# A fused window attention and maxout FFN: the hand-listed order of all steps is replaced by another one

## Chip, cores and metric

The kernel runs on one NeuronCore of a Trainium2 chip. The metric is the device time of one execution in microseconds; of several executions the median is taken. Engines are called PE (TensorE), DVE (VectorE), ACT (ScalarE), POOL (GpSimd) and SP (SyncE, which only issues transfers here).

## The reference

```python
def _attn_ref(q, k, v):                  # 8 batches, 8 heads, 576 positions, 64 wide
    ...
    scores = scale * np.matmul(q, k.transpose(0, 1, 3, 2))
    rel = pos[:, None] - pos[None, :]
    mask_plain = (rel >= 0) & (rel < window)                                  # heads 0 to 3, window 32
    mask_dil = (rel >= 0) & (rel < window * dilation) & (rel % dilation == 0) # heads 4 to 7, dilation 4
    ...
    scores = scores - np.max(scores, axis=-1, keepdims=True)
    attn = np.exp(scores)
    attn = attn / (np.sum(attn, axis=-1, keepdims=True) + 1e-09)
    return np.matmul(attn, v).astype(np.float32)

def _moe_ref(x, w1, w2, w3, w_out):      # x: 4608 tokens x 512; w: 512 x 768; w_out: 768 x 512
    h = np.maximum(np.maximum(x @ w1, x @ w2), x @ w3)
    return (h @ w_out).astype(np.float32)
```

The attention's output, with the heads side by side, is the x of the FFN.

## The kernel before

Attention works on units of one batch and two heads (32 units). The first eight (`early`, from line 601) use blocks of 32 rows, the other 24 (`attention` and `behind`, from line 888) blocks of 64. A unit goes: loads, scores on PE (L649 or L922), maximum and mask on DVE (L677, L960), exponential on ACT (L692, L972), sums, reciprocal, normalization (a two-operand product W times sm on POOL or DVE, L488), 32x32 transposes on DVE (L741, L1026), values on PE (L760, L1082), and copies of the result out of PSUM.

The FFN takes 4608 tokens in six tiles (`TILES`: 512, 512, 768, 768, 1024, 1024). Every fp32 operand is split into a high part in fp32r, copied by ACT or POOL (L456, L458), and a low part, subtracted by DVE or POOL (L488); a product is then three matmuls. The two first tiles (`plain`, L1551 and L1490) use the weights as they come; the four later ones (`fast`, L1793, and `turned_down`, L1357) use a scheme of seven products of half matrices instead of eight, whose operands are sums and differences of blocks (`changed`, L488 again) and whose weight sums are made once (`sums_of`, `down_sums`), stored to HBM (`kept_up`, `kept_d`) and loaded again as they are used (L1753, tile `wup_a<-kept_up`). Weights arrive as 512 KB loads (`st<-in_w_up_dram`, step `weight`), and each is taken apart by POOL or DVE (L554), ACT (L549), DVE (L560), a copy and a subtraction. Lines that are helpers are `copy` (L456 ACT, L458 POOL, L460 DVE) and `tt` (L488), which makes all two-operand work on DVE and POOL.

All this is put down as 3121 steps (`Plan.add`), each with the engines that may do it, its dependences and its buffers. Their order is not worked out by the kernel: `Plan.order` reads it from the string `SEQUENCE` (line 60), one number for each step, the step's place in the order of `add`. A letter behind a number (a, d, p) is the engine ACT, DVE or POOL where it isn't the step's first choice; an `f` is a filler, one bf16 matmul on a block of zeros (L2016) that only keeps PE busy. Steps are issued in that order, so the order on every engine, and on SP's queue of transfers, is the order of the string. An engine does its steps in that order and no other. `SLOTS` fixes which buffer each step uses. `Plan.issue` also makes each of the first 36 loads wait until no more than 2 MB of loads before it are under way.

Steps that the text speaks of by number:

- 163, 181: values of the first two units on PE; 209: a score block; 234: the first FFN matmul
- 60: load of weight tile 10, taken apart by 62, 63; 48, 54, 72, 42: loads of tiles 8, 9, 12, 7; 576: load of q and k for the score block 578
- 401, 403, 405: parts of a weight sum on DVE; 119: low part of a down weight on DVE; 140: first part of a weight; 311: the maximum that frees a PSUM bank in the first tile
- 1106, 1113: low parts of the third tile's inputs on DVE; 1107, 1114: differences of its blocks on POOL; 531, 535: low parts of weight sums on POOL
- 1168: load of a weight sum in the third tile; 2106: load of q and k of a later unit, 592 KB
- 2136: the short normalization of a unit (64x192) on POOL; 1350, 1352: copies of the high parts that the P7 products of the third tile take; 1355: a low part for them; 1611, 1614, 2289: differences of 768 or 1024 columns for the next tile; 1612, 2293, 2297: copies of its inputs

Of the kernel before, what the change touches and what calls it, by code (L numbers as in the profile page):

```python
# [60 lines left out]
    "152 f 170 f 189 f 188 f f 150 f f f f 0 154 f 207 155 172 156 f f 6 173 f f f f 174 f f 2 1 153 f f 157 191 3 "  # L61
    "175 158 f 176 f 159 18 f f 12 f 160 192 177 f f 161 f 7 f 178 138 193 f f 8 162 171 194 209 179 9 195 10 163 24 "
    "180 f 11 14 f 190 f f 210 208 f 13 196 f 4p 144 f 164 211 f 168 5 166 165 212 169 167 151 181 19 197 213 20 36 "
    "214d 215 f 15 216 f 66 186 f 21 182 f f f 538 187 f 22 26 f 234 217 184 235 198 16 236 23 237 25 239 185 17 218 "
    "183 30 27 199 28p 225 243 223 78 245 367 219 247 224 221 227 238 220 248 244 366d 200 557 368d 222 370 228 246 "
    "203 205d 226 29 201 229 48 206 31 230 371d 251 249 202 32 540 204 42 369 33 233 376p 34 250 242 240 38 35 232 54 "
    "241 231 541 372p 378 252 253 254 373 256 257 255 258 260 37 261 259 262 264 72 39 44 374 263 377 265 43 40 45 60 "
    "559 49 41 50d 46 51 90 266 56 542 55 268 52p 267 57 126 543 382 269 375 47 58 544 270 61 62 272 383 108 271 63 "
    "273 576 53 59 274 560 67 68 276 561 73 84 64 277 275 80 379 69 545 278 74 70 546 75 280 96 65 562 539 547d 79 "
    "281 384 279 102 282 563 76p 81 386 578 71 86 284 85 387d 385 564d 283 77 285 388 87 82 390 286 91 92 114 83 88 "  # L70
    "597 288 98 97 287 132 389 93 289 565 579 94 290 104 392 391 99 292 393 580 100 291 293 548 103 399 395 294 95 "
    "581 120 394 105 89 109 296 396 295 106 598 297 582 110 747 412 107 298 398 577 116d 115 380 599 583d 381 299 566 "
    "584 111 300 600 122 301 117 101 585d 302 400 304 303 401d 121 305 118 128 123 127 306 601 402 124 308 129 125 "
    "307 130 309 403d 133 131 119d 310 139 408 312 134 410 140d 460 313 311 146 409 141 314 135 145 112 316 324 113d "
    "317 404 315 406 405d 318 602 749 147 414 411 320 567 148 142 407 136 603 549 325 319 321 586 558 415 322 137d "
    "149 328 550 143 552 329 551 554 553 556 417 330 323 604 555 587 336 416d 418d 326 419 331 594d 596 588 327p 332 "
    "420 595 591d 424 751 589 422 421 592 593 426 337 425 423 333 827 801 787 764 338 756 334 797 768 431 752 339 757 "
    "762 335 766 590 754 763 760 340 427 770 346 758 795 605 341 799 606 803 761 805 793 568 755 791 347d 753 432 829 "
    "789 342 607 748 430 571 569 343 771 570 759 348 572 776 356 344d 434 349 769 435d 575 608 804 433d 573d 767 440p "
    "777 765 574 350 609 617d 773 615d 796 357 351 436 612d 616 352 794 438 774 437d 800 353 442 775d 441 439 831 354 "  # L80
    "806 772 443 611 792 429 802 447 355 358 790 842 846 788 345 838 359 613 847 428 848 798 834 360 750 832 844 446d "
# [2019 lines left out]
```

## Time and profile before

| | us |
|---|---|
| median of 3 runs | 635.98 (634.64 to 637.69) |
| the profiled execution | 637.17 |
| its span, first to last instruction | 635.4 |
| PE, DVE, ACT, POOL busy | 621.5, 507.8, 312.8, 227.1 |
| mean granted clock of PE | 0.997 |

A wait of PE shows in two ways: as idle time with the name of what ended it, and inside the busy time, since the ends of matmuls are modelled; the distance between the starts of matmuls shows both. A wait of DVE or POOL that begins when the instruction has been started is part of that instruction's duration.

### The profile page before, as it was taken

The page shows a single profiled execution, that of the slowest core. Times are in us where ns is not written, and L with a number is a line of the kernel's source. Part 1 is how long each engine was busy: PE and PEld are TensorE (multiplying, and loading weights), DVE is VectorE, ACT ScalarE, POOL GpSimd, SP SyncE. Part 2 cuts the span into 40 slices and gives each one's busy share as a digit, 9 for nine tenths or more (in the row PEclk, how much of TensorE's full clock was granted, in tenths as well). Part 3 has the DMA queues.
Part 4 walks back from the last instruction along what each step waited for, and adds up shares of the span by engine and source line. Part 5 has one row for each costly group of instructions (what it writes and reads, how often), then busy time and mean ns, then how long its engine had stood idle before and what let it go on. Part 6 is the DMA issues. An engine that isn't in the chain of part 4 may idle for free.

```text
span 635.4 us, 16084 instructions
## 1 busy us (share of the span) xinstructions
PE 621.5 (98%) x6025; PEld 530.1 (83%) x6025; DVE 507.8 (80%) x1368; ACT 312.8 (49%) x935; POOL 227.1 (36%) x266
## 2 busy tenths in 40 slices
PE   9898999999999999999999999999999999999997
PEld 4576868888888999898999999788888888888886
DVE  7868999999899998799889899987668854327575
ACT  3445547575766573665337457543135632212153
POOL 3779978989777411254102012520000000000000
PEclk9899999999999999999999999999999999999999
DMA  8999956996598998957979894565746366765533
GB/s 298 304 303 297 361 185 240 320 348 213 189 330 260 318 337 276 327 174 237 312 235 303 274 324 162 166 215 163 241 152 197 117 210 200 273 189 166 172 128 133
DMA packets 79710, 153.24 MB, mean 241 GB/s; under 512 B 7952, under 2 KB 26384, under 8 KB 79632
## 3 DMA queue, kind: packets, MB, share of 16 engines
q1 hardware_dynamic: 79488, 151.94, 72.1%
q8 instruction: 48, 0.79, 0.5%
q14 instruction: 30, 0.25, 0.1%
q10 hardware_dynamic: 144, 0.26, 0.1%
HBM read 123.08 MB, written 29.10 MB: 240 GB/s over the span
## 4 chain that ended last, share of the span: by engine, by line
PE 80%; DVE 8%; DMA 8%; issue 2%; POOL 1%; ACT 1%; SPq 0%; DVEq 0%; POOLq 0%; ACTq 0%
PE ffn L1793 46%; PE ffn L1357 12%; PE ffn L1551 10%; PE ffn L1490 4%; DMA st<-in_w_up_dram 4%; PE pair L922 3%; PE pair L1082 3%; DVE hs_all L488 2%; DVE wup_a L488 2%; DMA kept_up<-wup_a 1%; PE ffn L2016 1%; DMA wup_a<-kept_up 1%; DMA fk<-in_qk_p_dram 1%; DMA fk<-in_qk_d_dram 1%; DVE PT L1026 1%
## 5 line engine op out<-in xcount | busy, mean ns | idle before, releaser
L1793 PE MATMUL ffn<-wup_a 128*128 128x384 f32 (+1 forms) x1188 | 236.2, 356 | 1.9 <-DMA wup_a<-kept_up 1.1
L1793 PEld LDWEIGHTS ffn<-wup_a 128*128 128x128 f32 x1188 | 211.4, 188 | 21.5 <-DVE wup_a L488 2.4
L1551 PE MATMUL ffn<-xs,wup_a 128*128 128x512 f32 x408 | 97.5, 395 | 2.6 <-DVE hf L488 2.5
L1551 PEld LDWEIGHTS ffn<-xs,wup_a 128*128 128x128 f32 x408 | 75.7, 188 | 20.3 <-DVE hf L488 3.8
L488 DVE TENSOR_TENSOR hf<-ffn,hf 128x512 f32<-128x512 f32 (+1 forms) x96 | 60.0, 632 | 25.3 <-PE ffn L1793 22.3
L1026 DVE STREAM_TRANSPOSE PT<-W 32x256 f32<-32x256 f32 (+2 forms) x192 | 77.1, 401 | 3.3 <-POOL W L488 0.2
L972 ACT ACTIVATE W<-W,mx 128x96 f32<-128x96 f32 (+2 forms) x180 | 65.7, 367 | 10.3 <-DVE mx L960 9.8
L996 POOL TENSOR_SCALAR sm<-sm 128x8 f32<-128x8 f32 (+2 forms) x48 | 12.4, 257 | 118.8 <-ACT W L972 72.8
L456 ACT COPY ffn<-ffn 128x384 f32<-128x384 f32 (+1 forms) x32 | 16.6, 520 | 68.3 <-PE ffn L1793 52.7
L1357 PE MATMUL ffn<-hs_all,wdn 128*128 128x512 f32 (+1 forms) x228 | 49.5, 365 | 0.8 <-DVE hs_all L488 0.7
L456 ACT CAST hs_all<-hf 128x384 fp32r<-128x384 f32 (+4 forms) x55 | 32.2, 589 | 33.3 <-PE ffn L1357 17.1
L1357 PEld LDWEIGHTS ffn<-hs_all,wdn 128*128 128x128 f32 x228 | 41.2, 188 | 6.4 <-DVE hs_all L488 1.3
L1793 PE MATMUL ffn<-wup_a,wdn 128*128 128x512 f32 x192 | 46.1, 391 | 0.0
L488 DVE TENSOR_TENSOR hs_all<-hf,hs_all 128x384 fp32r<-128x384 f32 (+3 forms) x55 | 39.0, 721 | 7.9 <-ACT hs_all L456 6.8
L488 POOL TENSOR_TENSOR W<-W,sm 128x768 f32<-128x768 f32 (+2 forms) x33 | 38.5, 1173 | 15.1 <-DVE sm L1001 14.5
L488 POOL TENSOR_TENSOR hf<-hf 128x256 f32<-128x256 f32 (+1 forms) x41 | 41.6, 1020 | 5.6 <-DVE hf L488 2.2
L1793 PEld LDWEIGHTS ffn<-wup_a,wdn 128*128 128x128 f32 x192 | 35.8, 188 | 7.6 <-DVE wup_a L488 0.2
L1357 PE MATMUL ffn<-hs_all,wup_a 128*128 128x384 f32 (+1 forms) x198 | 39.2, 352 | 0.8 <-DVE hs_all L488 0.8
L456 ACT COPY u<-ffn 128x384 f32<-128x384 f32 (+1 forms) x35 | 18.5, 530 | 42.9 <-PE ffn L1793 42.1
L458 POOL TENSOR_SCALAR hs_all<-PT 128x512 fp32r<-128x512 f32 x1 | 0.6, 621 | 106.8 <-PE ffn L1357 106.8
L1357 PEld LDWEIGHTS ffn<-hs_all,wup_a 128*128 128x128 f32 x198 | 35.0, 188 | 3.8 <-DVE hs_all L488 1.6
L1490 PE MATMUL ffn<-wdn,hs_all 128*128 128x512 f32 x144 | 34.9, 395 | 0.2 <-DVE hf L488 0.2
(207 smaller groups left out, 1051.8 us busy)
## 6 DMA issues: line engine op xcount, KB each, us to landing
wup_a<-kept_up SPq DMA_DIRECT2D x198, 256.0 KB, 4.4
st<-in_w_up_dram SPq DMA_DIRECT2D x18, 512.0 KB, 5.3
kept_up<-hf SPq DMA_DIRECT2D x36, 256.0 KB, 3.7
wup_a<-kept_d SPq DMA_DIRECT2D x36, 256.0 KB, 5.1
wdn<-kept_up SPq DMA_DIRECT2D x32, 256.0 KB, 3.7
k<-in_qk_d_dram SPq DMA_DIRECT2D x12, 648.0 KB, 6.3
k<-in_qk_p_dram SPq DMA_DIRECT2D x12, 592.0 KB, 6.0
later<-kept_up SPq DMA_DIRECT2D x22, 256.0 KB, 4.0
```

Source lines behind the costliest of these rows:

```text
L456: nc.scalar.copy(dst, src)
L488: (nc.vector if eng == "dve" else nc.gpsimd).tensor_tensor(dst, a, b, op=op)
L922: nc.tensor.matmul(banks[j].t[o : o + nq, 96 * m : 96 * m + nk], kb.t[d, q0 : q0 + nq], kb.t[d, k0 : k0 + nk], start=True, stop=True,)
L972: nc.scalar.activation(W.t[rows, a], W.t[rows, a], AF.Exp, bias=mx.t[rows, n : n + 1], scale=-1.0, accum_out=sm.t[rows, n : n + 1],)
L996: nc.gpsimd.tensor_scalar(d, d, 1.0, 1e-9, ALU.mult, ALU.add)
L1026: plan.add({"dve": dve(32 * n) + 0.02}, lambda _: nc.vector.transpose(dst(), src()), [*deps, blank], [W, PT])
L1082: nc.tensor.matmul(pv[z].t[64 * j : 64 * j + 64, q : q + c1 - c0], v.t[d, j, y], PT.t[d, 576 * j + 96 * x + c0 : 576 * j + 96 * x + c1], s ...
L1357: nc.tensor.matmul(bank[e].t[:, :n], weights(wz, e), hop.t[:, hz], start=opens and not q and not m, stop=q == nq - 1 and m == 2, skip_grou ...
L1490: nc.tensor.matmul(bank.t.rearrange("p (k n) -> p k n", k=2), hb.t[:, hz, f], wdn[f].t[:, :, wz], start=(f == 0 and m == 0), stop=(f == NF ...
L1551: nc.tensor.matmul(bank.t, wup[j][:, c // 2, wz, 128 * (c % 2) : 128 * (c % 2) + 128], xs[xz][:, c, first : first + n], start=(m == 0 and ...
L1793: nc.tensor.matmul(bank.t[:, :n], wb.t[:, w : w + 128], xop(o, n)[:, xz, c], start=start and not m and not c, stop=m == 2 and c == 1, skip ...
L2016: nc.tensor.matmul(idle.t.rearrange("p (n k) -> p n k", n=4), blank_b, blank_b.unsqueeze(1).broadcast_to([128, 4, 128]), start=True, stop= ...
```

## The change

The string `SEQUENCE` is replaced. The steps, their dependences, `SLOTS` and all other lines stay as they are. The new string lists the same 3121 steps and 45 fillers instead of 47. It comes from a search on simulated runs in which GpSimd's steps of every length and VectorE's two-operand steps wait for each other. Of the steps that may run on more than one engine some change it, which the letters tell: 22 go from POOL to DVE, 13 from POOL to ACT, 14 from DVE and 7 from ACT to POOL, 20 from ACT to DVE, 11 from DVE to ACT. POOL has 237 steps instead of 251, DVE 1136 instead of 1119, ACT 690 instead of 693. On PE the order is nearly the same: beyond two places only steps of the first 30 us, the score blocks 578 (four steps later), 599 (three later) and 1512 (three earlier) move. The diff, cut to the lines that hold the steps named here (first lines before, then lines after):

```diff
@@ -58,139 +58,139 @@
 
 
...
-    "152 f 170 f 189 f 188 f f 150 f f f f 0 154 f 207 155 172 156 f f 6 173 f f f f 174 f f 2 1 153 f f 157 191 3 "
-    "175 158 f 176 f 159 18 f f 12 f 160 192 177 f f 161 f 7 f 178 138 193 f f 8 162 171 194 209 179 9 195 10 163 24 "
-    "180 f 11 14 f 190 f f 210 208 f 13 196 f 4p 144 f 164 211 f 168 5 166 165 212 169 167 151 181 19 197 213 20 36 "
-    "214d 215 f 15 216 f 66 186 f 21 182 f f f 538 187 f 22 26 f 234 217 184 235 198 16 236 23 237 25 239 185 17 218 "
...
-    "241 231 541 372p 378 252 253 254 373 256 257 255 258 260 37 261 259 262 264 72 39 44 374 263 377 265 43 40 45 60 "
-    "559 49 41 50d 46 51 90 266 56 542 55 268 52p 267 57 126 543 382 269 375 47 58 544 270 61 62 272 383 108 271 63 "
-    "273 576 53 59 274 560 67 68 276 561 73 84 64 277 275 80 379 69 545 278 74 70 546 75 280 96 65 562 539 547d 79 "
-    "281 384 279 102 282 563 76p 81 386 578 71 86 284 85 387d 385 564d 283 77 285 388 87 82 390 286 91 92 114 83 88 "
-    "597 288 98 97 287 132 389 93 289 565 579 94 290 104 392 391 99 292 393 580 100 291 293 548 103 399 395 294 95 "
...
-    "307 130 309 403d 133 131 119d 310 139 408 312 134 410 140d 460 313 311 146 409 141 314 135 145 112 316 324 113d "
...
-    "1098 1094 536 530 727 1103 1121 720 728 532 1104 1112 729 1512 1465 1105 1107p 1466 730 1106 1096 1180 535p 1934 "
-    "1108 1523 1517 1128 1573 1529 1513 1182 1109 1530 531p 1181 1518 1184 1494 1183 1114p 1463 537 533 1493 1186 "
-    "1498 1126 1519 1509 1188 1113 1187 1132 1520 1130 1524 1190 1525 1185 1115 1571 1531 1563 1192 1569 1135 1191 "
...
-    "1333 1598 1272 1162 1999 1599 1275 1164 1274 2006 1165 1968 1170 2016 2003 2005 1276 1277 2106 2023 2063 1167 "
-    "2073 2019 2017 1279 1168 2067 1278 2025 1348 2004 1281 1280 1967 2064 1970 1283 1176 2065 2077 1282 2078 1285 "
...
-    "2135 1338 1392 2156 1339 1380 2136 1395 1340 1393 1379 1341 1396 1343 1342 1394 1344 1397 1345 1609 1400 1346 "
-    "1350p 1399 1349 1398 1401 1351 1352p 1610 1402 1354 1353 1611p 1619 1355 1407 1405 1372 2148 1403 1408 1634 1374 "
-    "1373 2032 1632 2161 1614p 1375 1409 1629 1376 2163 1625 1377 1626 1414 1381 1410 1624 1612p 1412 1627 1415 1383 "
...
-    "1910 1882 2287 2658 1920 2281 1918 1887p 1921 1889 1916 1919 2666 1888 2295 2696 1883 2671 2288 1891 1890 2289p "
-    "1922 1892 2739 1927 1925 1923 1928 2751 2290 2292 1929 2291 2293p 2365 2311 1932 2296 1930 1912 1926 2367 2366 "
-    "2294 2660 2369 2674 2755 2368 2297p 2745 2672 2299 2371 2673 2315 2705 2300 2312 2697 2747 2741 1917 2757 2373 "
...
+    "152 f 170 f 188 f f f 150 f f f f 0 154 189 f 207 155 172 156 f f 157 173 f f 2 f 6 1 f 174 f f f 158 f 175 12 "
+    "191 3 159 160 176 161 f f 153 f 192 f 171 f f 177 f 193 f 8 7 f 138 f 162 f 194 f 4p f f 9 209 151 18 178 195 10 "
+    "179 11 24 163 14 180 13 208 5 f 210 144 f 164 f 168 f 166 f 211 196 f 165 212 169 20 190 167 181 197 19 213 21 "
+    "214 66 f 215 f 15 22 216 f f 538 182 f 186 23 234 25 183 26 184 217 16 225 235 198 236 54 187 239 237 27 218 17 "
...
+    "376p 372 253 60 254 256 38 257 255 258 373d 260 37 261 377 259 262 264 90 39 378 44 265 263 43 374 542 49 559 "
+    "375 50d 40 56 72 51 266 41 45 55 268 267d 46 84 62 57 269 52p 47 58 576 270 560 53 61 272 543 382d 273 383 271 "
+    "78 63 274 379 68 544 64 276 126 59 65 277 275 67 561 545 73 278 74 381 546 69 96 547 280 279 539 102 75 562 281 "
+    "384 70 282 79 386 71 80 284 85 283 86 76 114 285 385d 597 387 87 286 81 92 388 288 563 392 390 91 120 389d 578 "
...
+    "401d 133 134 129 312 119d 139 130 311 313 403d 601 314 408 404 140d 410 316 409 141 406 142 317 315 113d 411 145 "
...
+    "725 1094 1092 1098 720 1102 726 1512 1103 1104 727 1107p 1105 1934 1513 1529 1123 728 1466 1096 1112 1461 729 "
+    "1106 1180 730 531p 1494 1108 1182 1573 1130 1517 1523 1530 1109 1181 533 1184 1183 1131 1114p 1493 1574 1514 "
+    "1186 1465 1132 1518 1463 1509 1527 1188 1936 1113 1187 1492 1569 1190 1185 1115 535p 1525 1498 1192 1191 1519 "
...
+    "1598 1275 1604 745 1320 1602 1600 1599 1166 1333 1605 1168 1277 2005 1169 1999 1167 2016 1276 1278 2003 1274 "
+    "2006 1348 1279 2106 2021 2069 1937 2023 2063 2073 1281 1170 2025 2067 2077 2074 2065 2078 2019 2033 1283 1280 "
...
+    "1344 1397 1345 1349 1346 1400 1350 1609 1401 1352 1351 1398 1353 1399 1402 1632 1610 1354 2032 1407 1355 1372 "
+    "1373 1408 1634 1374 1403 1619 2153 1405 1409 1376p 2150 1406 1375 1626 2037 1414 2161 1381 2136 1410 1636 2162 "
+    "1377 1411 1415 1383 1382 1631 1412 1625 1416 1384 1385 1627 1611 1630 1421 2310 2159 1612 1386 1633 1422 2157 "
+    "1629 2163 2160 1417 1635 2154 1419 2146 1423 1614 1687 1613 1426 2148 2164 2007 1620 1615 2168 1618 1424 1688 "
...
+    "2305 1915 1881 2658 2613 2287 1882 1910 2295 1920 1883 1887 1921 2288 1889 1922 1891 1890 2297 1918 2696 1888 "
+    "1919 2666 1916 2307 2289 2615 1927 1892 2290 1923 1928 2292 1929 2291 2365 1932 2311 1925 2293 2296 1926 2367 "
...
```

## Rows read from the trace of the kernel before

**Rows 1.** The page: busy time, share of span and instructions of each engine

```profile
PE 621.5 (98%) x6025; PEld 530.1 (83%) x6025; DVE 507.8 (80%) x1368; ACT 312.8 (49%) x935; POOL 227.1 (36%) x266
```

**Rows 2.** Waits of TensorE: releaser, us in total, times, longest

```profile
PE ffn L1551 <- DVE hf L488: 2.5, 2, 1.6
...
PE ffn L1357 <- DVE hs_all L488: 1.5, 2, 0.8
PE ffn L1793 <- DMA wup_a<-kept_up: 1.1, 1, 1.1
...
PE ffn L1793 <- DVE wup_a L488: 0.8, 3, 0.3
```

**Rows 3.** Groups by shape on GpSimd: count, busy, mean ns

```profile
L488 POOL TENSOR_TENSOR W<-W,sm 64x192 f32<-64x192 f32 x11 | 9.9, 902 | 7.1 <-DVE sm L1001 6.9
```

**Rows 4.** Timeline, GpSimd, 276 to 292 us: start, duration, operation [idle before]

```profile
278.41 4.83 POOL L488 TENSOR_TENSOR W<-W,sm 64x192 f32<-64x192 f32 x1 [0.63 <-DVE sm L1001]
283.21 0.98 POOL L458 TENSOR_SCALAR hs_all<-hf 128x384 fp32r<-128x384 f32 x2
285.55 2.08 POOL L488 TENSOR_TENSOR freed<-freed,raw 128x768 f32<-128x768 f32 x1 [1.36 <-DVE freed L488]
```

**Rows 5.** Timeline, VectorE, the same stretch

```profile
278.19 0.53 DVE L488 TENSOR_TENSOR hs_all<-freed,hs_all 128x384 fp32r<-128x384 f32 x1
...
282.33 0.54 DVE L488 TENSOR_TENSOR freed<-freed,hf 128x384 f32<-128x384 f32 x1
...
285.86 2.19 DVE L488 TENSOR_TENSOR hs_all<-freed,hs_all 128x384 fp32r<-128x384 f32 x1
```

**Rows 6.** Timeline, TensorE, 283 to 298 us

```profile
282.71 4.62 PE L1357 MATMUL ffn<-hs_all,wup_a 128*128 128x384 f32 x23
288.10 1.15 PE L1357 MATMUL ffn<-hs_all,wup_a 128*128 128x384 f32 x5 [0.78 <-DVE hs_all L488]
289.13 0.41 PE L1357 MATMUL ffn<-hs_all,wdn 128*128 128x384 f32 x1
290.21 6.76 PE L1357 MATMUL ffn<-hs_all,wdn 128*128 128x384 f32 x35 [0.68 <-DVE hs_all L488]
296.81 1.21 PE L1793 MATMUL ffn<-wup_a 128*128 128x384 f32 x6
```

**Rows 7.** Chain that ended last: start, duration, work, three stretches of TensorE

```profile
21.97 3.50 PE ffn L2016 x8
...
299.68 26.20 PE ffn L1793 x150
...
517.50 84.32 PE ffn L1793 x372
```

**Rows 8.** Timeline, TensorE, 397 to 406 us

```profile
397.99 3.77 PE L1793 MATMUL ffn<-wup_a 128*128 128x512 f32 x14
402.08 4.16 PE L1793 MATMUL ffn<-wup_a 128*128 128x512 f32 x17 [0.33 <-DVE wup_a L488]
```

**Rows 9.** Timeline, GpSimd, 392 to 406 us

```profile
393.43 2.64 POOL L488 TENSOR_TENSOR raw<-raw 128x1024 f32<-128x1024 f32 x1 [1.16 <-DVE raw L488]
```

**Rows 10.** Timeline, VectorE, 78 to 90 us

```profile
78.30 1.78 DVE L488 TENSOR_TENSOR wdn<-c,wdn 128x512 fp32r<-128x512 f32 x1
...
80.66 0.68 DVE L488 TENSOR_TENSOR hf<-ffn,hf 128x512 f32<-128x512 f32 x1
```

**Rows 11.** Timeline, GpSimd, 47 to 60 us

```profile
47.33 0.64 POOL L554 TENSOR_SCALAR c<-st 128x512 uint32<-128x512 uint8 x1 [1.44 <-DMA st<-in_w_up_dram]
```

**Rows 12.** Timeline, TensorE, 47 to 60 us

```profile
55.62 1.02 PE L649 MATMUL pair<-fk 64*32 64x64 f32 x80 [0.67 <-DMA fk<-in_qk_d_dram]
```

**Rows 13.** Timeline, SyncE queue, 244 to 257 us

```profile
249.30 5.10 SPq L1753 DMA_DIRECT2D wup_a<-kept_up  x5
```

**Rows 14.** Stretches: busy us of each engine, clock, DMA share, GB/s

```profile
16.00:32.00 16.00, 14.02 (x363) 9.21 (x346) 14.14 (x29) 6.99 (x18) 11.99 (x17) 0.89 0.94 304
192.00:208.00 16.00, 15.55 (x172) 14.45 (x171) 15.71 (x58) 11.91 (x41) 13.57 (x9) 1.00 0.81 268
```

225 rows, old and new, of the table SEQUENCE are left out of this document.

## The prediction

> **What bounds the kernel now.** I read the page's busy line first, then TensorE's waits, then the timelines of the places where TensorE waits, and last the order of the steps in the diff. PE is busy for 621.5 of 635.4 us, DVE for 507.8, POOL for 227.1 [rows 1]: PE sets the end, and since the change gives PE the same matmuls, all that a new order can do is to take away or add time in which PE isn't at its full pace. That pace is to be seen in dense stretches: 150 matmuls of 384 columns in 26.20 us are 0.1747 each, 372 of 512 columns in 84.32 us are 0.2267 each [rows 7]. The second stretch, from 517 to 602 us, has nothing to give. PE's own list of waits has some six microseconds on three lines of DVE and one load [rows 2].
>
> Why DVE is late at these places is the point. A short normalization on POOL (64x192) took 4.83 us at 278.41 [rows 4], while the eleven of its kind have a mean of 902 ns, so the other ten took (9.9 - 4.83) / 10 = 0.51 us [rows 3]. In these 4.83 us DVE went through nine instructions one behind another, all with two operands in SBUF, the first at 278.19 and the last at 282.33, which took 0.53 and 0.54 us [rows 5]. The other way round, a subtraction on DVE of the same shape took 2.19 us at 285.86 [rows 5], while a difference on POOL ran from 285.55 for 2.08 us [rows 4]: DVE stood until POOL had ended at 287.63. So a step of POOL and a two-operand step of DVE don't run at once, whichever comes second waits, and a short step of POOL can wait as long as a long one. This is what the search behind the new order is told.
>
> **The change part by part.** Every step stays; the order on each queue and the engine of 87 steps change. I go through the places where PE loses time now and ask what the new string lists there. First those where the clash itself makes the loss.
>
> At 284 to 297 us. Behind the 4.83 us normalization (step 2136) POOL had two copies, 1350 and 1352, which ended at 284.19 [rows 4]; the P7 products need them. Then the differences 1611 and 1614 on POOL hold DVE's 1355. From 282.71 to 296.81 PE makes 23 + 5 + 1 + 35 = 64 matmuls in 14.10 us [rows 6]; at 0.1747 they are 11.18, so 2.9 us are lost. The new string gives 1350 and 1352 to ACT and 1611 and 1614 to DVE, behind the products that they held, and lists 2136 ten PE steps further back, where DVE's splits for P7 are done. What it adds there are two 768-column differences on DVE, which stand behind all that P7 and P2 need. I take the 2.9 as gone; next late is the load behind them, which isn't waited for now.
>
> At 398 to 402 us: 14 matmuls take 402.08 - 397.99 = 4.09 us [rows 8], at 0.2267 they are 3.17; 0.9 lost. Before it a difference of 1024 columns on POOL (step 2289) takes 2.64 us [rows 9] and two copies of POOL (2293, 2297) follow. All three leave POOL (2289 to DVE, the copies to ACT), and POOL has two short copies left in these 15 us, far ahead. 0.9 gone, less what 2289 costs DVE: between nothing (DVE stood for it while POOL did it) and the 2.64 us that it took on POOL; I take nothing, since DVE no longer waits for it.
>
> At 79 to 81 us PE waits 2.5 - 1.6 = 0.9 us [rows 2] for step 311, the maximum that frees a PSUM bank, 0.68 us at 80.66 [rows 10]. Ahead of it on DVE stand 403, then 119 with 1.78 us [rows 10], both held by POOL, then 140. The new string puts 403 and 140 behind 311. 0.9 gone.
>
> At 194 to 202 us PE waits three times for subtractions into `wup_a`, 0.8 us with the one of 0.33 at 402.08 [rows 2, 8], so 0.5 here. The new string puts single-operand work (maxima, transposes) beside the differences 1107 and 1114 of POOL, but DVE is busy 15.71 of 16 us there [rows 14]. I take 0.2 of the 0.5.
>
> Sum of the clashes: 2.9 + 0.9 + 0.9 + 0.2 = 4.9 us.
>
> Second, places where a load or the fill of the queues is late, which the change isn't about but moves all the same. Eight fillers after step 181 take 3.50 us, 0.44 each [rows 7], in a stretch whose granted clock is 0.89 [rows 14], that is, a part of it at the lower of two levels (1.2 of 2.4 GHz), after PE has stood still; the string has five there, 1.3 us less. The longer wait for a maximum in the first tile, 1.6 us [rows 2], goes back to weight tile 10, for which POOL waited 1.44 us at 47.33 [rows 11]; its load (60) now has 1536 KB less in front of it, some 5 us at the 304 GB/s of [rows 14]. The score block 578 waited 0.67 us for its load [rows 12], which has 1024 KB less in front, while the block comes four products later. The 1.1 us wait for `wup_a<-kept_up` [rows 2] follows a load that SP issued among five in 5.10 us [rows 13], behind the 592 KB of 2106; now 1168 stands in front of it. Together 1.3 + 1.6 + 0.7 + 1.1 = 4.7 us.
>
> I don't count these 4.7. Each is a place where one queue met one late load; the new order moves others back (the load of tile 6 now has 2640 KB more in front of it, tile 13 5592 KB more), and has 496 transfers to be late with. The bounds are 4.7 us gained, when none is late, and nothing, when as much appears elsewhere; the present order has 4.7 us of it on the chip, and these are the nearest rows there are, so I take nothing.
>
> Costs: DVE has 17 steps more. At 0.53 to 0.68 us (the two-operand step of 384 columns and that of 512 [rows 5, 10]) that is 9.0 to 11.6 us of DVE's 635.4 - 507.8 = 127.6 us of idle time [rows 1]; beside it DVE stands less in clashes. I take nothing. Two fillers fewer are in the 1.3 above. The three score blocks that move on PE take the same time where they are now.
>
> What a clash costs the one that waits can be read in two ways. DVE's 2.19 us ended 0.4 us after POOL's step of 2.08 us: one instruction of the other engine was waited for. POOL's 4.83 us went on through nine instructions of DVE [rows 4, 5]. The sum above goes by the second reading where POOL is the one that waits. The Trainium skill, SBUF — State Buffer, section "SBUF: two separate sides", has the first: it calls the port pair that VectorE and GpSimd share an exclusive lock, held for the whole instruction of the one that starts first. DVE's 2.19 us agree with that sentence, POOL's 4.83 us don't; by it the sum would be that of rival 3.
>
> **The sum.** Against the profiled execution: 637.17 - 4.9 = 632.3 us. That run lies 1.2 us above the median, so for the median 635.98 - 4.9 = 631.1 us.
>
> **The rivals.**
>
> 1. The queues' lateness goes as well: 4.7 us more, 631.1 - 4.7 = 626.4. For it speaks that each of the four places is visibly mended in the string; against it, that any order of so many transfers meets some.
>
> 2. The clashes go, but DVE takes their place. It is at 15.71 of 16 us from 192 to 208 [rows 14], and it gets 1611, 1614 and 2289. Then PE waits for DVE's length, not for its clashes; the 2.9 us and the 0.2 stay, and 0.9 + 0.9 are won: 634.2. Against it: the differences stand behind what PE needs next.
>
> 3. POOL waits for one instruction of DVE and no more, and the rest of the 4.83 us has another cause that stays. Then of the 2.9 us only what DVE's 1355 stood is won, 2.19 - 0.53 = 1.7 us [rows 5]: the sum is 4.9 - 2.9 + 1.7 = 3.7, the time 632.3. This is the section on the exclusive lock of SBUF — State Buffer in the Trainium skill, taken at its word. The nine DVE instructions without a gap beside the 4.83 us speak against it.
>
> 4. Slower: DVE sets the end in stretches where it is full. The place is 192 to 208 us, where DVE is busy 15.71 of 16 us [rows 14], and the stretches like it; the price is the added work itself, 9.0 to 11.6 us for 17 steps; it decides as soon as nearly half of it, and no gain, lands where DVE is already full: 635.98 + 4.5 = 640.5. Against it: POOL gives 14 steps away, some of them 2 us long, and DVE's own stretched instructions get shorter.
>
> 5. The string doesn't do on the chip what it lists: the engines run out of step with the list, so clashes that it avoids come back elsewhere. Then the 4.9 us go and come: 636.
>
> **How the numbers follow.** Forecast 0.50, of which almost all lies under 632.8; rival 1 0.14; rival 3 0.05, half to each side of 632.8; rival 2 0.12; rival 5 0.10; rival 4 0.09. 0.5% is 3.2 us, about what a measurement of this kernel can tell from no change: faster is below 632.8, slower above 639.2. Faster: 0.45 + 0.14 + 0.03 = 0.62; slower 0.09; same 0.29. The range reaches from rival 1 (626.4) to just above rival 5, 636.5, and leaves out rival 4 and the tails. The forecast's own range is 629 to 633.
>
> **What would show it.** Right: no POOL step of 64x192 above 1.5 us, POOL idle from 393 to 402 us, the P7 products of the third tile at 0.1747 us a matmul, no wait of PE for `hs_all` there, and DVE's busy time not higher although it has 17 steps more, since its stretched instructions are gone. Wrong: new waits of PE for DVE where DVE is full, new waits on `st<-in_w_up_dram` or `kept_up` in the first 100 us, or a later start of the first FFN matmul (step 234) than now.

## The result, and the profile after

The changed kernel takes 629.47 us (median of 4 runs, 627.39 to 630.49) beside 635.33 for the kernel before in the same comparison: a ratio of 0.9897, 95% interval 0.986 to 0.9934, that is 4.2 to 8.9 us less. The ratios here and below are worked out from all runs and are not the quotients of the medians, which lie 5.9 us apart here. Run again later it was 628.99 beside 636.22, 0.989 (0.9855 to 0.9926). The forecast was 631.1 in a range of 626.4 to 636.5, and faster at 0.62. The profiled execution took 629.65 us, its span is 627.9.

The page's busy line after, which answers to [rows 1]:

```profile
PE 618.7 (99%) x6023; PEld 530.4 (84%) x6023; DVE 499.4 (80%) x1385; ACT 311.9 (50%) x932; POOL 203.0 (32%) x252
```

VectorE has 17 instructions more and is busy 8.4 us less: its durations held time in which it stood for GpSimd. TensorE has its two fillers less and no other matmul less.

The waits of TensorE after (releaser, us in total, times, longest), which answer to [rows 2]:

```profile
PE ffn L760 <- DMA hf<-in_fv_d_dram: 1.6, 1, 1.6
PE ffn L1551 <- DVE hf L488: 1.1, 1, 1.1
...
PE ffn L1793 <- ACT u L456: 0.4, 1, 0.4
PE ffn L1793 <- DMA wup_a<-kept_up: 0.2, 1, 0.2
```

The waits for `hs_all` and for VectorE's `wup_a` are gone, and so is the wait of 1.1 for `kept_up`; the 0.2 for `kept_up` in this list stands at another place, near 427 us. New is a wait of 1.6 us for a load of the first units, and of the two waits for `hf` one of 1.1 us stands at another place (48.7 us).

The stretch where the prediction saw 2.9 us lost, GpSimd and VectorE after, 276 to 290 us, which answer to [rows 4, 5]:

```profile
282.19 0.51 POOL L458 TENSOR_SCALAR hs_all<-hf 128x384 fp32r<-128x384 f32 x1 [9.64 <-PE ffn L1357]
...
283.24 0.50 POOL L488 TENSOR_TENSOR W<-W,sm 64x192 f32<-64x192 f32 x1
```

```profile
279.87 0.55 DVE L488 TENSOR_TENSOR hs_all<-freed,hs_all 128x384 fp32r<-128x384 f32 x1
...
285.54 0.95 DVE L488 TENSOR_TENSOR freed<-freed,raw 128x768 f32<-128x768 f32 x1
...
288.56 0.95 DVE L488 TENSOR_TENSOR raw<-raw,freed 128x768 f32<-128x768 f32 x1
```

Step 2136 takes 0.50 us where it took 4.83; the low part 1355 takes 0.55 where it took 2.19; the differences 1611 and 1614 take 0.95 each on VectorE, 2.08 and 2.03 on GpSimd before.

TensorE after, 283 to 300 us and 396 to 406 us, which answers to [rows 6, 8]:

```profile
282.98 6.40 PE L1357 MATMUL ffn<-hs_all,wdn 128*128 128x384 f32 x36
289.21 1.21 PE L1793 MATMUL ffn<-wup_a 128*128 128x384 f32 x6
...
395.84 3.56 PE L1793 MATMUL ffn<-wup_a 128*128 128x512 f32 x15
399.24 4.24 PE L1793 MATMUL ffn<-wup_a,wdn 128*128 128x512 f32 x18
```

36 matmuls go from 282.98 to 289.21, 0.173 us each, the dense pace of [rows 7]; 15 of 512 columns go from 395.84 to 399.24, 0.2267 each. Both places are dense now.

**Where the time went.** The same step of TensorE was looked up in both traces; the number is its start after less its start before, so a change from one step to the next is time won (below zero) or lost in between.

| stretch of before, us | steps of PE | won or lost in after |
|---|---|---|
| 0 to 73 | to 305 | -1.4 |
| 73 to 89 | 305 to 328 | -1.7 |
| 89 to 219 | 328 to 1222 | -0.2 |
| 219 to 284 | 1222 to 1407 | -1.3 |
| 284 to 295 | 1407 to 1422 | -3.0 |
| 295 to 398 | 1422 to 2365 | +0.6 |
| 398 to 406 | 2365 to 2375 | -1.0 |
| 406 to the end | 2375 to 3118 | +0.4 |

These are single executions, and the first stretch of any of them is not a property of the order alone, as the experiments showed: eight profiled executions with the old early order (the kernel before and seven experiments) started step 300 between 2.3 us earlier than the first trace of before and level with it, on average 1.1 earlier. The 1.2 us between 1222 and 1289 (the wait of 1.1 for `wup_a<-kept_up` in [rows 2]) goes in part without the new order too: against the first trace of before, the eight executions with the old order there win 0.7 on average (two of them nothing), the four with the new one 1.1.

### The profile page after: what moved, and what is told of

Its sections match the earlier page's. It is cut to its first block, busy times and chain, and to the rows that moved or that the text cites. A ratio compares the mean times of both kernels' runs of the same rounds, so it can differ in the third digit from the quotient of the medians.

```text
span 627.9 us, 16042 instructions
## 1 busy us (share of the span) xinstructions
PE 618.7 (99%) x6023; PEld 530.4 (84%) x6023; DVE 499.4 (80%) x1385; ACT 311.9 (50%) x932; POOL 203.0 (32%) x252
## 4 chain that ended last, share of the span: by engine, by line
PE 88%; DMA 6%; DVE 3%; POOL 1%; ACT 1%; issue 1%; SPq 0%; DVEq 0%; ACTq 0%
PE ffn L1793 47%; PE ffn L1357 16%; PE ffn L1551 13%; PE ffn L1490 3%; PE pair L922 3%; PE pair L1082 3%; PE ffn L2016 1%; DMA kept_up<-hf 1%; DMA wup_a<-kept_up 1%; DMA fk<-in_qk_d_dram 1%; DMA hf<-in_fv_d_dram 1%; DMA kept_d<-dc 1%; DMA st<-in_w_up_dram 1%; DVE hf L488 1%; PE pair L760 1%
## 5 line engine op out<-in xcount | busy, mean ns | idle before, releaser
L488 DVE TENSOR_TENSOR hf<-ffn,hf 128x512 f32<-128x512 f32 (+1 forms) x96 | 60.9, 636 | 36.6 <-PE ffn L1793 33.8
L1357 PE MATMUL ffn<-hs_all,wdn 128*128 128x512 f32 (+1 forms) x228 | 48.8, 363 | 0.0
L1357 PEld LDWEIGHTS ffn<-hs_all,wdn 128*128 128x128 f32 x228 | 41.3, 188 | 4.8
L488 POOL TENSOR_TENSOR W<-W,sm 128x768 f32<-128x768 f32 (+2 forms) x33 | 34.6, 1051 | 25.4 <-DVE sm L1001 24.2
L1357 PE MATMUL ffn<-hs_all,wup_a 128*128 128x384 f32 (+1 forms) x198 | 38.8, 350 | 0.0
L488 DVE TENSOR_TENSOR hs_all<-hf,hs_all 128x384 fp32r<-128x384 f32 (+3 forms) x56 | 36.0, 651 | 2.0 <-POOL hs_all L458 1.0
L1357 PEld LDWEIGHTS ffn<-hs_all,wup_a 128*128 128x128 f32 x198 | 35.0, 188 | 2.6 <-POOL hs_all L458 0.2
L960 DVE CUSTOM_DVE_ANT_0 W<-pair,steps 128x96 f32<-128x96 f32 (+1 forms) x158 | 34.5, 250 | 1.9 <-PE pair L922 1.1
```

Of the source, the lines that this page charges most:

```text
L488: (nc.vector if eng == "dve" else nc.gpsimd).tensor_tensor(dst, a, b, op=op)
L960: nc.vector.tensor_tensor_reduce(W.t[rows, a], banks[j].t[rows, 96 * m : 96 * m + nk], mask_of(m)[rows], -0.125, 3e38, ALU.add, ALU.min, m ...
L1357: nc.tensor.matmul(bank[e].t[:, :n], weights(wz, e), hop.t[:, hz], start=opens and not q and not m, stop=q == nq - 1 and m == 2, skip_grou ...
```

## The experiments

In the experiments with the kernel's work only `SEQUENCE` is edited; a few lines of the file more ahead of the steps make L488 an L490 or L491 there and L1357 an L1359 or L1360.

**1. Halves.** The old string up to step 1233 (near 224 us), then the new one, each without what the other has listed:

```diff
  <old> 1951 1152 1941 1224 1151 1230 1233
+ <new, what is left> 1147 1985 1946 1939 1952 1153 ...
```

> The old order up to the FFN product 1233 (224 us in the trace of before, 221 in that of after), then the new order of all steps that are left. Clash theory: the early stalls stay as before, the waits at 254, 284 to 297 and 398 to 402 us go, as in the trace of after, where the distance to before grows from 3.3 us at 1222 to 7.6 at 2455: 4.2 us less than before, some 631. Rival, the gain comes from an earlier start and other loads: next to nothing, within 1 us of before.

Measured: 633.67 us beside 635.55, ratio 0.996 (0.9941 to 0.9979), 2.5 us with 1.3 to 3.7 in the interval, less than the 4.2 that were expected. In the trace 3.0 us go between 1407 and 1422 and 1.0 between 2365 and 2375, as expected; but 0.6 and 1.2 come back at steps 1908 and 1915. The only waits of TensorE from 255 us to the end:

```profile
PE ffn L1360 <- DMA wup_a<-kept_d: 1.5, 2, 1.1
```

In the fourth tile the new order's loads of stored weight sums come too late for two products, 0.4 us at 380.08 and 1.1 at 384.51. The four profiled executions with the new order there lose between 0.2 and 1.8 us at these two steps (0.2 in the first trace of after); those with the old order lose nothing. It is the longest new wait that the late part of the new order has; beside it the two traces of after have 0.2 and 0.3 us for `kept_up`, at different places.

The other half, the new string up to 1233 and then the old one:

```diff
  <new> 1943 1231 1983 1323 1951 1230 1233
+ <old, what is left> 744p 1549 1150 1975 1148 1152 ...
```

> The new order up to the FFN product 1233, then the old order of what is left. Clash theory: only the early gain, 3.3 us as the two traces stand apart at 1222, some 632, and the 4.83 us normalization, the stall of 2.9 us at 284 to 297 us and that of 0.9 us at 398 to 402 us come back, shifted by 3.3 us. Rival, the gain comes from an earlier start and other loads: 5 us or more, since PE stays ahead of the queues later on.

Measured: 632.52, ratio 0.9945 (0.9923 to 0.9968), 3.5 us (2.0 to 4.9). Nothing is won between 1407 and 1422 nor at 2365 to 2375, as it should be. Step 1222 starts 2.6 us earlier than in the first trace of before.

The three executions of the new early order (after twice, and this half) start step 1222 at -3.3, -3.1 and -2.6, on average 3.0 earlier; the eight of the old one at 0, -2.3, 0.3, -1.1, -2.0, -1.4, 0.4 and -1.4, on average 0.9. So by the traces the early order is worth 2.1 us, less than the 3.3 that a comparison of the first two traces shows; the runs of this half (2.0 to 4.9) leave room for either. All of it lies behind step 305 (73 us): each of the three wins 1.0 by step 316, 0.7 from there to 328, between 1180 and 1222 0.3 on average. At step 305 they stand at -1.4, -0.4 and -1.0, the old ones at -1.1 on average: no gain shows there from the loads and the fill of the queues.

**2. One stretch.** The new order only between steps 1301 and 1705 (263.5 to 308 us):

```diff
  <old> 2110 2060 1297 2036 2062 2079 1301
+ <new> 1937 1299 ... 1427 2089 1705
  <old, what is left> 2166 1639 2167 ...
```

> The old order, with the new one in its place between the FFN products 1301 and 1705 alone (263.5 to 308 us in the trace of before; 268 places of the list). Clash theory: 2.9 us less, some 632.5, the 64 matmuls from the P7 products on take 11.2 instead of 14.1 us, and no POOL step of 64x192 takes over 1.5 us. Rival, DVE is full there and its length sets the pace: under 1 us less.

Measured: 632.93, ratio 0.9953 (0.9931 to 0.9976), 3.0 us (1.5 to 4.4). In its trace exactly 3.00 us go between 1407 and 1422, and nothing is given back later.

**3. The normalization alone.** The prediction put the loss there down to step 2136, whose 4.83 us keep the copies 1350 and 1352 from TensorE, and to the differences that hold 1355. Here only 2136 is moved, ten steps of TensorE back:

```diff
- 2156 1339 1380 2136 1395 1340
+ 2156 1339 1380 1395 1340
...
- 1377 1626 1414 1381 1410
+ 1377 1626 1414 2136 1381 1410
```

> The old order with one step moved: the normalization 2136 (4.83 us on POOL) ten PE steps further back, behind product 1414. The copies 1350 and 1352 stay on POOL, the differences 1611 and 1614 too. Clash theory: the copies run some 3.5 us earlier, the P7 products lose only what 1611 holds of 1355 (1.7 us): a loss of 1.5 to 2 us instead of 2.9 from 282.7 to 296.8 us. Rival, one instruction is the most a step waits and the 4.83 us has another cause: 2136 takes as long at its new place and the loss stays near 2.9.

Measured, in one run: 633.82 us, of which nothing comes from this place: 1422 starts as long after 1407 as before. GpSimd, from 278 us on, and below it VectorE's steps 1355 and 1375:

```profile
278.32 2.14 POOL L461 TENSOR_SCALAR hs_all<-hf 128x384 fp32r<-128x384 f32 x2 [3.80 <-PE ffn L1360]
281.82 2.09 POOL L491 TENSOR_TENSOR freed<-freed,raw 128x768 f32<-128x768 f32 x1 [1.36 <-DVE freed L491]
283.99 2.04 POOL L491 TENSOR_TENSOR raw<-raw,freed 128x768 f32<-128x768 f32 x1
285.97 0.83 POOL L491 TENSOR_TENSOR W<-W,sm 64x192 f32<-64x192 f32 x1
```

```profile
282.13 2.20 DVE L491 TENSOR_TENSOR hs_all<-freed,hs_all 128x384 fp32r<-128x384 f32 x1
...
286.54 1.47 DVE L491 TENSOR_TENSOR hs_all<-hf,hs_all 128x384 fp32r<-128x384 f32 x1
```

2136 takes 0.83 us at its new place. But the copy takes its part: of the 2.14 us the first copy has 1.67, because the copy too stands until VectorE's chain pauses (at 279.61), and the second 0.51. VectorE got to 1355 only 0.5 us earlier, and 1355 then stood for the differences as long as ever. The half microsecond lasts as far as product 1415 and is lost there: its low part 1375 took 1.47 us beside 2136 at its new place and the copy behind it, and 1.00 in the kernel before:

```profile
290.25 1.00 DVE L488 TENSOR_TENSOR hs_all<-hf,hs_all 128x384 fp32r<-128x384 f32 x1
```

**4. The copies alone,** and **5. the differences alone.**

```diff
- 1346 1350p 1399 ... 1351 1352p 1610
+ 1346 1350 1399 ... 1351 1352 1610
```

> The old order; the copies 1350 and 1352 go from POOL to ACT at their places in the list, 2136 stays where it is. As the prediction had it, the copies behind the 4.83 us normalization make the P7 products late: the loss between product 1407 and 1422 falls from 3.0 us by 1 us or more. Second theory, after moving 2136 alone left that loss at 3.0 us: only DVE's subtraction 1355 held by the POOL difference 1611, and 1614 behind it, make the loss: it stays at 3.0 us within 0.3.

Measured, in one run: 634.84 beside 634.48; between 1407 and 1422 1.2 us are won. GpSimd and, below it, VectorE:

```profile
277.39 7.11 POOL L491 TENSOR_TENSOR W<-W,sm 64x192 f32<-64x192 f32 x1 [0.63 <-DVE sm L1004]
284.46 1.84 POOL L491 TENSOR_TENSOR freed<-freed,raw 128x768 f32<-128x768 f32 x1
```

```profile
283.58 0.55 DVE L491 TENSOR_TENSOR hs_all<-freed,hs_all 128x384 fp32r<-128x384 f32 x1
284.05 1.00 DVE L491 TENSOR_TENSOR du<-ffn,du 128x384 f32<-128x384 f32 x2
```

VectorE no longer pauses for the copies, for which it waited 0.88 us in the kernel before:

```profile
283.75 0.85 DVE L488 TENSOR_TENSOR hs_all<-hf,hs_all 128x384 fp32r<-128x384 f32 x1 [0.88 <-POOL hs_all L458]
```

And the product takes 7.11 us: it ends 0.37 us after the last step of VectorE with two SBUF operands (283.58 + 0.55 = 284.13), when VectorE has come to `du<-ffn,du`, whose first operand lies in PSUM. In before it ended 283.24 - 282.87 = 0.37 after VectorE's last step ahead of a pause.

```diff
- 1353 1611p 1619 ... 2161 1614p 1375
+ 1353 1611 1619 ... 2161 1614 1375
```

> The old order; the 768-column differences 1611 and 1614 go from POOL to DVE at their places in the list, everything else stays. Second theory: 1355 takes 0.55 us instead of 2.19, the subtractions for the next products too, and the loss between 1407 and 1422 falls from 3.0 us to under 1 us, though DVE has two steps of 0.95 us more. As the prediction had it: 2136 keeps the copies late and the loss falls by no more than 1.7 us.

Measured, in one run: 633.88 beside 634.48; 1.0 us is won there. VectorE and, below it, GpSimd:

```profile
283.61 0.94 DVE L491 TENSOR_TENSOR freed<-freed,raw 128x768 f32<-128x768 f32 x1
284.48 0.55 DVE L491 TENSOR_TENSOR hs_all<-freed,hs_all 128x384 fp32r<-128x384 f32 x1
```

```profile
276.16 4.83 POOL L491 TENSOR_TENSOR W<-W,sm 64x192 f32<-64x192 f32 x1 [0.63 <-DVE sm L1004]
280.97 0.98 POOL L461 TENSOR_SCALAR hs_all<-hf 128x384 fp32r<-128x384 f32 x2
```

1355 takes 0.55 again, and 1611 on VectorE 0.94 where GpSimd took 2.08; 2136 keeps its 4.83 us and the copies still end late.

**6. Copies and differences together.**

```diff
- 1350p ... 1352p ... 1611p ... 1614p
+ 1350 ... 1352 ... 1611 ... 1614
```

> The order of before with four steps put elsewhere and nothing else: the copies 1350 and 1352 from GpSimd to ScalarE and the differences 1611 and 1614 from GpSimd to VectorE. Moved by itself the first pair gave 1.2 us between PE steps 1407 and 1422 and the second 1.0, of the 3.0 that the whole new order of that stretch gives. Theory: the loss has two causes that stand one behind the other, the copies that stand behind the product 2136 on GpSimd's queue, and the differences that hold VectorE's 1355; with both gone 2.2 to 3.0 us go there, so 632.4 to 633.2 for a median of before of 635.4, and 2136 may take as long as it did. Rival: the third cause is the product itself, whose lock slows nothing of PE's but keeps VectorE's splits late; then the pair gives no more than the larger of the two, 1.2 us, 634.2.

Measured: 633.42 beside 636.22, ratio 0.9963 (0.9944 to 0.9982), 2.4 us (1.1 to 3.6). Between 1407 and 1422 2.14 us go, about the sum of 1.2 and 1.0: two causes one behind the other, the rival's 1.2 is out. GpSimd's product there, and the waits of TensorE from 276 to 300 us:

```profile
276.03 7.97 POOL L491 TENSOR_TENSOR W<-W,sm 64x192 f32<-64x192 f32 x1 [0.63 <-DVE sm L1004]
```

```profile
PE ffn L1360 <- DVE hs_all L491: 0.2, 1, 0.2
```

The product takes longer than ever, and no wait of TensorE goes back to it. What is left to the 3.0 us, 0.86, does not lie at 1355: that step starts 1.0 us after 1407 (0.01 in the kernel after), but product 1409, which takes it, starts 2.08 us after 1407 in both. It lies at products 1415 (0.5) and 1421 (0.3). VectorE ends their low parts 1375 and 1382 4.69 and 7.10 us after the start of 1407, and their second matmuls start at 4.74 and 7.15; in the kernel after they start at 4.33 and 6.41. The string of before lists the differences 1611 and 1614 ahead of these two low parts, the new one behind them. That their place makes the 0.86 is read from the traces; no run moves them in the list alone.

**7. The steps ahead of 399 us alone.**

```diff
- 1890 2289p 1922 ... 2291 2293p 2365 ... 2368 2297p 2745
+ 1890 2289 1922 ... 2291 2293 2365 ... 2368 2297 2745
```

> The old order; the difference 2289 goes from POOL to DVE and the copies 2293 and 2297 from POOL to ACT, at their places in the list. Clash theory: the products 2365, 2367 and 2369 lose 0.9 us less, as in the new order. Rival, DVE is full there and 2289 costs what it frees: the loss of 0.9 us stays or grows by up to 1.2 us, the time of such a step on DVE.

Measured, in one run: 635.2 beside 634.48; between 2365 and 2375 0.9 us go, as in after. VectorE there:

```profile
392.82 1.22 DVE L490 TENSOR_TENSOR raw<-raw 128x1024 f32<-128x1024 f32 x1
...
396.85 3.48 DVE L490 TENSOR_TENSOR wup_a<-raw,wup_a 128x1024 fp32r<-128x1024 f32 x3
```

Step 2289 takes 1.22 us on VectorE where GpSimd took 2.64 [rows 9], and the three low parts 3.48 together where they took 4.32.

**8. The clash by itself.** None of the kernel's work; a product of 64x192 on GpSimd, issued beside chains of VectorE steps.

> Not the kernel: none of its work is done, the output is filler. Eight sections, one behind another. In each, POOL starts one step (a 64x192 product of SBUF operands, a 128x384 copy, or a 128x384 product) when DVE has finished a first step, while DVE goes on through 0, 2, 4 or 8 subtractions of 128x384 with both operands in SBUF, or 8 transposes, that wait for nothing. If the one that waits goes on after one instruction of the other: POOL's product takes some 0.5 us alone and 1.0 to 1.1 us beside 2, 4 or 8 subtractions alike. If it waits as long as the other engine's instructions follow without a gap, as the 4.83 us row reads: some 1.4, 2.3 and 4.2 us beside 2, 4 and 8. Beside transposes 0.5 us in both. DVE's first subtraction that comes while POOL's 128x384 product runs waits for its end.

Measured, GpSimd's product alone and beside 2, 4 and 8 subtractions, then VectorE's chain of eight:

```profile
4.71 0.58 POOL L47 TENSOR_TENSOR prod_pool<-prod_first 64x192 f32<-64x192 f32 x1 [4.28 <-DVE prod_first L37]
...
7.30 0.83 POOL L47 TENSOR_TENSOR prod_pool<-prod_first 64x192 f32<-64x192 f32 x1 [1.26 <-DVE prod_first L37]
...
10.13 0.83 POOL L47 TENSOR_TENSOR prod_pool<-prod_first 64x192 f32<-64x192 f32 x1 [1.27 <-DVE prod_first L37]
...
13.46 0.83 POOL L47 TENSOR_TENSOR prod_pool<-prod_first 64x192 f32<-64x192 f32 x1 [1.75 <-DVE prod_first L37]
```

```profile
13.30 4.22 DVE L26 TENSOR_TENSOR prod<-a 128x384 f32<-128x384 f32 x8
```

A copy of 128x384 took 0.75 us beside eight subtractions and 0.51 alone; beside eight transposes of VectorE the product took 0.58, as alone. So here the product waits for one instruction of VectorE with two SBUF operands, however many stand behind it. That spoke for the reading of rival 3 and left the kernel's 4.83 us without a cause, so the forms were varied one at a time.

> None of the kernel's work: seven sections, in each a GpSimd product of 64x192 elements beside nine VectorE steps of two SBUF operands, issued back to back. They differ from the kernel's place at 278.41 by one thing each: 'full' has the kernel's forms (the product's second operand repeats one number 96 times, the product is let go by a reciprocal, VectorE's steps are alternately a split that writes fp32r and a difference in place); 'same' has the plain subtractions of the earlier microbenchmark, 'plain' a product whose second operand repeats nothing, 'after' a product let go by a two-operand step in place of the reciprocal, 'psum' has as its fifth VectorE step one whose first operand lies in PSUM, 'high' works in partitions 64 to 127, 'none' has no VectorE step beside it. Theory: in the kernel's form the product waits until VectorE comes to a pause or to a step that doesn't read two SBUF operands: 4.3 to 4.8 us in 'full', about 2.4 in 'psum', 0.5 to 0.6 in 'none', and the section that comes down to 0.8 names the form that decides. Rival: one VectorE step is all that it waits for, 0.8 to 1.0 us in all sections, and the 4.83 and 7.11 us in the kernel have a cause that no such section holds.

Measured, GpSimd's product in the seven sections, then rows of VectorE:

```profile
6.12 4.48 POOL L66 TENSOR_TENSOR full_w<-full_w,full_sm 64x192 f32<-64x192 f32 x1 [5.68 <-DVE full_sm L58]
11.87 4.49 POOL L66 TENSOR_TENSOR same_w<-same_w,same_sm 64x192 f32<-64x192 f32 x1 [1.26 <-DVE same_sm L58]
17.62 4.57 POOL L66 TENSOR_TENSOR plain_w<-plain_w,plain_sm 64x192 f32<-64x192 f32 x1 [1.26 <-DVE plain_sm L58]
23.65 0.75 POOL L66 TENSOR_TENSOR after_w<-after_w,after_sm 64x192 f32<-64x192 f32 x1 [1.47 <-DVE after_sm L60]
29.24 2.15 POOL L66 TENSOR_TENSOR psum_w<-psum_w,psum_sm 64x192 f32<-64x192 f32 x1 [4.84 <-DVE psum_sm L58]
34.75 0.88 POOL L66 TENSOR_TENSOR high_w<-high_w,high_sm 64x192 f32<-64x192 f32 x1 [3.37 <-DVE high_sm L58]
40.46 0.50 POOL L66 TENSOR_TENSOR none_w<-none_w,none_sm 64x192 f32<-64x192 f32 x1 [4.83 <-DVE none_sm L58]
```

```profile
9.70 0.54 DVE L39 TENSOR_TENSOR hs<-f,hs 128x384 fp32r<-128x384 f32 x1
...
23.96 0.86 DVE L37 TENSOR_TENSOR hf<-hf,f 128x384 f32<-128x384 f32 x1
...
30.48 0.54 DVE L37 TENSOR_TENSOR hf<-hf,f 128x384 f32<-128x384 f32 x1
31.05 0.56 DVE L43 TENSOR_TENSOR f<-ffn,f 128x384 f32<-128x384 f32 x1
```

The kernel's 4.83 us is there, 4.48 in `full`, and none of the operands' forms makes it: plain subtractions and a product without repeated numbers give 4.49 and 4.57. It ends 10.60 - 10.24 = 0.36 us after the chain's last step, and in `psum` 31.39 - 31.02 = 0.37 after the last step ahead of the one with a PSUM operand. So in one and the same kernel a GpSimd step either gets in behind one step of VectorE (0.75, 0.88; VectorE's next step then takes 0.86) or behind the whole chain. It got in when a two-operand step of VectorE let it go (`after`, and all sections of the first microbenchmark) and waited through the chain when a reciprocal did, in the lower partitions; in the upper ones it got in although a reciprocal let it go, but there VectorE's chain began 0.19 us after the reciprocal's start and not 0.08. What decides is not settled by this.

**9. A mended order.** The two longest waits of after, each taken away by one move: the maximum 271 ahead of 382, which stands for a store, and load 153 ahead of load 12.

```diff
- 543 382d 273 383 271
+ 543 273 383 271 382d
...
- 175 12 191 ... 153 f 192
+ 175 153 191 ... 12 f 192
```

> The order of after with two places mended: VectorE's maximum 271 stands ahead of 382, which waits for a store of wup_a's space near 47.3, and load 153 stands ahead of load 12 on SyncE's queue. Theory: in the kernel after, PE waits 1.1 us at 48.7 for a tile that VectorE makes behind 382, and 1.6 us for load 153 of an early value block; both lie on the path, since PE was late for nothing else there, so 1.0 to 2.5 us go and the median comes 1 to 2 us below that of after beside it. Rival: the stretch up to 60 us hangs on the loads and stores as a whole, and a mended wait comes back as another wait for a load a few us later: within 0.5 us of after.

> The kernel after once more, beside the mended one and on the same chip: 628 to 630.5 us, a ratio to before of 0.986 to 0.993 as at first; and in its trace the stretch up to PE step 1222 shows whether its 3.3 us there against the first trace of before are the order's or vary from execution to execution (seven executions of the old early order stood between -2.3 and +0.4, two of the new at -2.6 and -3.3): theory -2.2 to -3.5, rival any value from -2.3 to 0.4.

Measured side by side: 628.67 (628.07 to 629.54, ratio to before 0.9885, 0.9862 to 0.9909) and 628.99 (0.989, 0.9855 to 0.9926). The mended order isn't told apart from after. The first waits of the mended one, and below them those of after in its second trace:

```profile
PE pair L763 <- issue: 1.7, 1, 1.7
PE pair L763 <- DVE xs L491: 1.2, 1, 1.2
```

```profile
PE pair L760 <- issue: 2.0, 1, 2.0
...
PE pair L760 <- DVE xs L488: 0.8, 1, 0.8
```

In the second trace of after the two waits that were to be mended are not there in the first place; others of the same size stand among the values and the first matmuls. Step 1222 starts at -4.2 in the mended order, at -3.1 in the second trace of after (theory: -2.2 to -3.5). The rival had it: the median stays within 0.5 us of that of after, and waits of the same size stand elsewhere. That the start hangs on the loads as a whole is its reading, which these two traces bear out but do not isolate.

## Why the prediction was right, point by point

**The mechanism.** Each of the four places where the prediction saw a clash is mended. Only one gain that all executions of the new order show stands elsewhere, 0.7 us between 81 and 89 us, which had no term. Half of it falls at step 328, ahead of which TensorE waited for VectorE before and doesn't wait after; what makes the rest is open. The wait in the trace of before:

```profile
88.79 1.43 PE L1490 MATMUL ffn<-wdn,hs_all 128*128 128x512 f32 x5 [0.19 <-DVE hf L488]
```

| term | predicted | measured | by |
|---|---|---|---|
| 284 to 297 us | 2.9 | 3.0 | five traces with the new order there |
| 398 to 402 us | 0.9 | 1.0 (0.9 in experiment 7) | all late new orders |
| 79 to 81 us | 0.9 | 1.0 | all traces of the new early order |
| 194 to 202 us | 0.2 | 0.3 | the same |
| 81 to 89 us | 0 | 0.7 | the same |
| loads and fillers, start to 73 us | 0 | -0.1 | three new against eight old |
| the wait for `kept_up`, 219 to 256 us | 0 (with the row above 0 to 4.7) | 0.4 | four new against eight old |
| behind 295 us, elsewhere | 0 | -1.1 | +0.6 and +0.4 in the table above |

Measured terms: 3.0 + 1.0 + 1.0 + 0.3 + 0.7 - 0.1 + 0.4 - 1.1 = 5.2 us; predicted 4.9; the medians lie 5.9 apart (4.2 to 8.9 by the ratio), and 7.2 in the second comparison. The sum lies in the lower part of both, and a microsecond or two between traces and medians stays unexplained; the start varies by that much from execution to execution. That the sum comes so near to 4.9 is in part luck: three terms that the prediction did not have or put at nothing, 0.7, 0.4 and -1.1, cancel.

**The step that failed** is the chain of causes for the largest term. The prediction put the 4.83 us of 2136 first, with the copies behind it that the P7 products need, then the differences that hold 1355, and took the 2.9 us as gone without saying which makes how much. In the trace of before the products that wait for the copies lose 0.5 us: 1409 starts 2.55 us after 1407, and 2.08 in that of after. The other 2.5 fall at 1409 (1.1, for 1355), 1414 (1.0) and 1421 (0.4), whose low parts VectorE makes late. Moving 2136 alone gave nothing: the copies then stood for the same chain of VectorE, and the half microsecond that was won was lost again at 1415. The copies alone gave 1.2 (VectorE too had paused 0.9 us for them), the differences alone 1.0, both 2.1, and the last 0.9 goes, as the traces read, with the place of the differences in the list. With 2136 at 7.97 us the loss was 0.9, smaller than in any other run that lists this stretch in the old order, so the length of 2136 is not what TensorE pays for. The size was right since it was read off the distance between TensorE's matmuls [rows 6], which doesn't ask who is to blame.

**DVE at no cost** was right: 17 steps more, 8.4 us less busy, and the 24 us that GpSimd lost (227.1 to 203.0) were in part its own waits. The differences cost VectorE 0.95 and 1.22 us, less than half of what GpSimd took for them.

**Loads at nothing** was right for the sum and for the reason given: the named waits did go and others came, 1.6 us for load 153, up to 1.8 us for `kept_d` in the fourth tile.

**The rivals.** Rival 1 (626.4) needs the loads' lateness to go; it didn't. Rival 2 needs VectorE to be late where it is full; in the first trace of after TensorE waits nowhere for VectorE's `wup_a`, and the new late waits are for loads. Rival 3, that GpSimd waits for one instruction only, is refuted in this kernel by the 7.11 and 7.97 us of experiments 4 and 6, and yet holds in six sections of the microbenchmarks: both occur. The Trainium skill, SBUF — State Buffer, section "SBUF: two separate sides", has the port pair held for the whole instruction of the one that starts first. The 0.83 us beside two, four and eight subtractions agree with it; the 4.48 us, through nine instructions, do not, and here the measurement decides. Rival 4 (slower) and rival 5 are out: the string's order is seen on the engines, of the nine products of 64x192 left on GpSimd none takes more than 1.10 us, and the first FFN matmul starts 0.35 us earlier, which is less than its spread.

## What to carry to other kernels

Size a loss by the distance between the bound engine's instructions against its dense pace, and only then look for who made it; the causes stand one behind another, and an edit that takes away the first one named may win nothing. A short GpSimd step beside a long run of two-operand VectorE steps is one to move, to another engine or to where VectorE pauses or reads PSUM, if TensorE or VectorE waits for it or for what stands behind it on GpSimd; if neither does, its length cost TensorE nothing here (7.97 us in experiment 6). The long differences were shorter on VectorE (0.95 against 2.08 us), even though it had more to do then; they belong behind the low parts that TensorE needs next. Before a difference between two traces is explained, look at several executions of the same order: here the first 73 us vary by over 2 us in one and the same order.

## What the runs showed of the hardware that was not expected

A GpSimd product of 64x192 elements, 0.50 us by itself, took 4.48 to 7.97 us beside VectorE, and each time it ended 0.36 to 0.45 us after VectorE's last step with two SBUF operands, whether VectorE then paused or went on with a PSUM operand (0.37 in the kernel before and in experiment 4). A plain copy on GpSimd waits in the same way (1.67 us in place of 0.50 in experiment 3). The same product beside the same chain can also get in after one step (0.75 to 0.88 us), at VectorE's cost of 0.3 us. Which of the two happens is not settled: it got in where a two-operand step had let it go and, in the lower partitions, waited where a reciprocal had, but in the upper partitions it got in behind a reciprocal too.
